# w_out's rows placed on eight DMA engines, and 13 gMLP chunks instead of 20

## The chip, the cores and the metric

One NeuronCore of one Trainium2 chip runs the whole kernel. The metric is the device time of one execution in microseconds, as the median of several runs.

## What is computed

Two branches share one input `x` (4 sequences, one token each, 640 wide), and their results are added to it. Everything is bf16 at the borders.

```python
def _A_ref(x, k_cache, v_cache, wq, wo):             # 32 heads of 128, 4096 keys, 4 sequences
    q = (x @ wq).reshape(B, Sq, H, Dh).transpose(0, 2, 1, 3)
    scores = einsum('bhqd,bhkd->bhqk', q, k_cache) * Dh ** -0.5
    o = einsum('bhqk,bhkd->bhqd', softmax(scores), v_cache)
    return o.transpose(0, 2, 1, 3).reshape(B, Sq, H * Dh) @ wo
def _B_ref(x, w_in, w_sp, b_sp, w_out):              # w_in 640 x 1728, w_out 864 x 640
    z = gelu(x @ w_in); z1 = z[..., :Fh]; z2 = layernorm(z[..., Fh:])
    g = einsum('ts,bsf->btf', w_sp, z2) + b_sp[None, :, None]
    return (z1 * g) @ w_out
x = A_x; xn = layernorm(x)
return x + _A_ref(xn, A_k_cache, A_v_cache, A_wq, A_wo) + _B_ref(xn, B_w_in, B_w_sp, B_b_sp, B_w_out)
```

The caches are 134 MB each, so nearly all of the work is reading them.

## The kernel before

**Memory.** `kv` is one SBUF tile of five slots; a slot holds half of a unit of K or V. A unit is one sequence and eight heads: 64 KB on each of 128 partitions, 8 MB in all, so that there are 16 units of K and 16 of V, four of each to a group of heads (g = 0 to 3). Slots 0 to 2 first hold the small weights: `wq` (slots 0 and 1), `w_in` and the first part of `w_out` (slot 2), with the scratch of the layernorm, of q and of the gMLP behind them. `w_words` is a second tile; it takes the transposed K blocks (two buffers of 2048 words, `kT_t`), and at the start, in the same words, the rest of `w_out` (`w_rest`).

**Loads.** SP issues all large loads in one written order: `wq`, `w_in`, `w_out` (lines 126 and 127), two of the three pieces of the rest of `w_out` (line 133), then the units K0, K1, K2, K3, V0, K4, V1, K5 and so on (line 181, the list `seq`), with `wo` of group 0 behind K7 and the other groups' `wo` at the end (line 189). The fourth K unit of each group and the last V unit come in two parts. `place` gives each unit its slots: K0 slots 3 and 4, K1 0 and 1, K2 2 and 3, K3 4 and 0, V0 1 and 2, later V units 0 and 1. SP waits before each issue until the slots are free, and the loads behind wait with it.

**The rest of w_out.** `w_out` has 864 rows of 640. The first 384 lie on all 128 partitions, three rows (FA) to a partition. The other 480 are cut into the pieces of `PC`: first partition, last partition, rows to a partition n, and a count k, the outermost dimension of the source, which sets on how many DMA engines the load runs. Pieces 0 and 1 go out on SP's queue with k = 5 and 3, piece 2 on GpSimd's queue (POOL) with k = 2. The engines of a GpSimd load are consecutive ones behind those of the GpSimd load before it; the load `walk` (14 rows of 256 elements into a tile that nothing reads) only moves that place on by seven. `tc.issue_after` keeps the order of the two. The unused partitions of `w_rest` are set to zero by the memset of line 128, for which the pieces wait.

**The gMLP at the start.** The layernorm of x (lines 205 to 222; GpSimd squares in L211), q (L301) and z = x w_in (L338 to L343, PSUM tiles `z_ps` and `zr_ps`) follow one another. `z` is laid out so that its columns match the rows of `w_out` on each partition and each chunk, a Gelu to each piece (L357 to L360). Then GpSimd and VectorE compute the inner layernorm and the gate (L371 to L390), and PE multiplies chunk by chunk (L403): FC = FA + FR = 20 chunks of 128 rows, two matmuls each, into `proj`, where the attention's output is added later. A chunk's matmul reads one row of `w_out` of every partition.

**Attention.** For each K unit VectorE transposes eight blocks into `w_words` (L425) and PE makes the scores (L436). Behind a group's fourth K unit come softmax, the fill of the block-diagonal weights `Zb` (L469 to L473), and for each V unit 64 matmuls (L509). The output projection with `wo` (L552) ends with the pieces of the last group's `wo`, then two small stores.

Of the kernel before, what the change touches and what calls it, by code (L numbers as in the profile page):

```python
# [1 line left out]

# [9 lines left out]
F32 = mybir.dt.float32  # L12
# [4 lines left out]
def kernel(  # L17
# [19 lines left out]
    nc = tc.nc  # L37
    P = 128
    B, Sq, D = A_x.shape
    _, H, Sk, Dh = A_k_cache.shape  # L40
    assert Sq == 1 and B == 4 and Dh == P and D % P == 0
    DC = D // P
# [11 lines left out]
    G = HG * B  # L54
    F2 = B_w_in.shape[1]
    Fh = F2 // 2
    FA = 3
    FR = 17
    nf = FA * P

    PC = ((0, 20, 10, 5), (32, 44, 12, 3), (60, 68, 17, 2))
    f_at = [nf]
    for p0, p1, n, _ in PC:
        f_at.append(f_at[-1] + (p1 - p0) * n)
    assert Fh == f_at[-1]
    FC = FA + FR
    NOUT = A_wo.shape[1]
# [11 lines left out]
    ps_o = ctx.enter_context(tc.tile_pool(name="ps_o", bufs=2, space=bass.MemoryType.PSUM))  # L79
# [6 lines left out]
    def misc_ps(shape, dtype):  # L86
        misc_ctr[0] += 1
        return ps_m.tile(shape, dtype, tag="misc", name=f"misc{misc_ctr[0]}")
# [5 lines left out]
    n_p = (2 * TC + 1) * 16  # L94
    w_words = const.tile([P, max(2 * NKT + n_p, FR * NOUT // 2)], F32, name="w_words")
    kT_t = w_words[:, 0:2 * NKT].rearrange("p (i n) -> p i n", i=2)
    pT_t = w_words[:, 2 * NKT:2 * NKT + n_p].bitcast(BF16).rearrange("p (j r) -> p j r", r=32)

    def at_slot(i, n, off=0):
        return kv[:, i * SL + off:i * SL + off + n]  # L100
# [22 lines left out]

    w_out = at_slot(2, FA * NOUT, n_in).rearrange("p (c n) -> p c n", c=FA)

    nc.sync.dma_start(out=w_out[:, 0:2], in_=B_w_out[0:2 * P, :].rearrange("(p c) n -> p c n", p=P))
    nc.sync.dma_start(out=w_out[:, 2:3], in_=B_w_out[2 * P:nf, :].rearrange("(p c) n -> p c n", p=P))
    nc.vector.memset(w_words[:, 0:FR * NOUT // 2], 0.0)  # L128
    w_rest = w_words[:, 0:FR * NOUT // 2].bitcast(BF16).rearrange("p (c n) -> p c n", c=FR)

    def load_piece(eng, t):
        p0, p1, n, k = PC[t]
        return eng.dma_start(out=w_rest[p0:p1, 0:n].rearrange("p c n -> p (c n)"),
                             in_=B_w_out[f_at[t]:f_at[t + 1], :].rearrange("(r i c) n -> i r (c n)", i=k, c=n))

    NST = 256
    walk = const.tile([14, NST], BF16)

    load_piece(nc.sync, 0)
    load_piece(nc.sync, 1)  # L140
    sw = nc.gpsimd.dma_start(out=walk, in_=B_w_out[0:14, 0:NST].rearrange("(r i) n -> i r n", i=7))
    with tc.issue_after(sw.ins):
        load_piece(nc.gpsimd, 2)

    NB = 32 * FC
    z_at = n_in + FA * NOUT

# [72 lines left out]
    xnT = const.tile([P, DC, 32], BF16)  # L220
# [43 lines left out]
    for q in range(4):  # L264
        nc.gpsimd.tensor_copy(out=SelE[32 * q:32 * q + 32, :, q % 2, :],
                              in_=b8[32 * q:32 * q + 32, 8:8 + HP, None].to_broadcast((32, HP, P // HG)))
# [10 lines left out]
                          in_=ident_f[:].rearrange("p (q x c) -> p q x c", q=2, c=C2))  # L277
# [12 lines left out]
    for hf in range(NH):  # L290
        nc.tensor.matmul(proj[0:32, 0:NO2], lhsT=ident_bf[:XR, 1 - hf:33 - hf],
                         rhs=x_bf[:, hf * NO2:(hf + 1) * NO2], start=(hf == 0), stop=False)
# [4 lines left out]
    for hf in range(2):  # L297
        for c in range(DC):
            for j in range(NG):
                n0 = j * HG * Dh + hf * 512  # L300
                nc.tensor.matmul(q4_ps[32 * j:32 * j + 32, hf * 512:hf * 512 + 512], lhsT=xnT[:, c, :],  # L301
                                 rhs=wq[:, c, n0:n0 + 512], start=(c == 0), stop=(c == DC - 1))
# [14 lines left out]
    w_z = w_in.rearrange("p c (a f) -> p c a f", a=2)  # L317
    z_ps = misc_ps([P, 2, FA, 32], F32)
    zr_ps = misc_ps([P, 2, 256], F32)


    z_in = [[], [], [], []]
    for t, (p0, p1, n, k) in enumerate(PC):
        src = w_z[:, :, :, f_at[t]:f_at[t + 1]]
        for q in range(p0 // 32, (p1 - 1) // 32 + 1):
            x0, x1 = max(p0, 32 * q), min(p1, 32 * q + 32)
            if x1 - x0 < p1 - p0:
                assert (x1 - x0) * k == p1 - p0
                src_q = src.rearrange("p d a (r i c) -> p d i a r c", i=k, c=n)[:, :, (x0 - p0) // (x1 - x0)]
            else:  # L330
                src_q = src
            z_in[q].append((t, x0 - 32 * q, x1 - 32 * q, src_q))
    z_of = [[sum((x1 - x0) * PC[t][2] for t, x0, x1, _ in z[:m]) for m in range(len(z) + 1)] for z in z_in]
    w_z2 = w_z[:, :, :, 0:2 * P].rearrange("p c a (q j i) -> p c q a i j", q=4, j=32)
    w_z1 = w_z[:, :, :, 2 * P:nf].rearrange("p c a (q j) -> p c q a j", q=4)
    for c in range(DC):
        for q in range(4):
            nc.tensor.matmul(z_ps[32 * q:32 * q + 32, :, 0:2], lhsT=xnT[:, c, :], rhs=w_z2[:, c, q], start=(c == 0), stop=False)  # L338
            nc.tensor.matmul(z_ps[32 * q:32 * q + 32, :, 2], lhsT=xnT[:, c, :], rhs=w_z1[:, c, q], start=False,
                             stop=(c == DC - 1))  # L340
        for q in range(4):
            for m, (_, _, _, src) in enumerate(z_in[q]):
                nc.tensor.matmul(zr_ps[32 * q:32 * q + 32, :, z_of[q][m]:z_of[q][m + 1]], lhsT=xnT[:, c, :], rhs=src[:, c],  # L343
                                 start=(c == 0 and m == 0), stop=(c == DC - 1 and m == len(z_in[q]) - 1))
    z_f = at_slot(2, 2 * 3 * NB, z_at).bitcast(F32).rearrange("p (a n) -> p a n", a=3)
    z_b = at_slot(2, 2 * NB, z_at + 6 * NB).rearrange("p (a n) -> p a n", a=2)
    zT = z_f[:, 0:2, :].rearrange("p a (i j) -> p a i j", j=32)
    nc.gpsimd.memset(z_f[:, 0:2, :], 0.0)
    nc.scalar.activation(out=zT[:, :, 0:FA, :], in_=z_ps[:], func=ACT.Gelu_apprx_tanh)
    for q in range(4):  # L350
        rows = slice(32 * q, 32 * q + 32)
        for m, (t, x0, x1, _) in enumerate(z_in[q]):
            p0, p1, n, k = PC[t]
            z = zr_ps[rows, :, z_of[q][m]:z_of[q][m + 1]]
            dst = zT[rows, :, FA:FA + n, x0:x1]
            if x1 - x0 < p1 - p0:
                nc.scalar.activation(out=dst, in_=z.rearrange("p a (x c) -> p a c x", c=n), func=ACT.Gelu_apprx_tanh)  # L357
            else:
                for a in range(2):
                    nc.scalar.activation(out=dst[:, a].rearrange("p c (i r) -> p c i r", i=k),  # L360
                                         in_=z[:, a].rearrange("p (r i c) -> p c i r", i=k, c=n), func=ACT.Gelu_apprx_tanh)
# [36 lines left out]
    for f0 in range(0, FC, 4):  # L398
        for hf in range(NH):
            for fc in range(f0, min(f0 + 4, FC)):  # L400
# [3 lines left out]
                                 rhs=(w_out[:, fc] if fc < FA else w_rest[:, fc - FA])[:, hf * NO2:(hf + 1) * NO2],  # L404
                                 start=(fc == 1 and hf == 0), stop=False)
# [156 lines left out]
    for i, item in enumerate(seq):  # L562
# [10 lines left out]
        g, b = divmod(u, B)  # L573
# [22 lines left out]
    for c, hf in ((0, 0), (1, 0), (0, 1), (1, 1), (2, 0), (2, 1)):  # L596
        p = min(c, 1)
# [49 lines left out]
```

## Time and profile before

| what | value |
|---|---|
| median of 3 runs | 663.61 us (663.38 to 663.67) |
| span of the profiled execution, first to last instruction | 661.8 us |
| its own launch time | not listed apart; 1.8 us lie between the span and the median |
| DMA: packets, bytes, mean rate | 7132, 282.60 MB, 427 GB/s |
| PE, VectorE, ScalarE, GpSimd busy | 43%, 57%, 11%, 11% |
| mean granted TensorE clock | 0.736 |
| PE's code fetches (q8 instruction) | 18, 0.29 MB |

Queue q1 in the profile is SP's, q10 ScalarE's, q0 GpSimd's; q8 and q14 bring instructions. The DMA row of the page gives the busy tenths of all 16 DMA engines in 40 slices of 16.5 us. In the chain of work each step is followed back to what released it. Beside the views, the trace holds a record for every DMA packet (queue, start, duration, bytes), though not its engine; where the text speaks of packet records, these are meant.

### The profile page before, as it was taken

Reading aid. Unit: us, or ns where it says so; the run is one execution under the profiler, and the core shown is the slowest. Engines: PE = TensorE matmul, PEld = TensorE weight load, DVE = VectorE, ACT = ScalarE, POOL = GpSimd, SP = SyncE. Lnnn points to the kernel's source line nnn. Section 1 sums busy time; section 2 is a strip of 40 time slices with the busy share of each in tenths; the row PEclk is TensorE's granted clock in tenths of the full one; section 3 lists DMA queues with packets and bytes.
Section 4 is the critical chain, followed back from the end, with each engine's and each line's share of the span. In section 5 each row is a group of like instructions: output and inputs, shape, how many; then the busy total and the mean of one; then the engine's idle time right before and its main releaser. Section 6 shows DMA issues by size and latency. Waiting matters only on the chain.

```text
span 661.8 us, 5507 instructions
## 1 busy us (share of the span) xinstructions
PE 286.8 (43%) x2291; PEld 107.4 (16%) x2291; DVE 377.1 (57%) x307; ACT 74.0 (11%) x143; POOL 70.1 (11%) x138
## 2 busy tenths in 40 slices
PE   0336555446052456234426065642607245541236
PEld 0221111112011122111102022210202112120113
DVE  5329989766191759718346196764619175971112
ACT  0300000340100000330200000070100000042200
POOL 4620000030200000130300000030110000002300
PEclk9868788669578596676858587665857768766678
DMA  9999999999999999999999999999999999999997
GB/s 370 457 429 428 427 442 437 440 421 428 421 440 433 440 415 446 425 437 436 437 432 432 429 418 437 446 433 440 425 420 436 437 436 417 456 420 437 419 420 289
DMA packets 7132, 282.60 MB, mean 427 GB/s; under 512 B 913, under 2 KB 1308, under 8 KB 1692
## 3 DMA queue, kind: packets, MB, share of 16 engines
q1 hardware_dynamic: 6968, 282.07, 98.9%
q8 instruction: 18, 0.29, 0.2%
q0 software_dynamic: 112, 0.18, 0.1%
q14 instruction: 6, 0.05, 0.0%
q10 hardware_dynamic: 28, 0.01, 0.0%
HBM read 282.25 MB, written 0.01 MB: 426 GB/s over the span
## 4 chain that ended last, share of the span: by engine, by line
DMA 75%; DVE 11%; issue 11%; PE 2%; DVEq 0%; SPq 0%
DMA kv<-in_A_k_cache_dram 59%; DVE w_words L425 11%; DMA kv<-in_A_v_cache_dram 10%; DMA kv<-in_A_wo_dram 4%; DMA kv<-in_A_wq_dram 3%; PE O L509 2%; PE S L436 0%; PE proj L552 0%; DVE o_q L604 0%; DVE o L600 0%; DVEq L425 0%; SPq L189 0%; DVE o_bf L615 0%; SPq L181 0%; PE last L552 0%
## 5 line engine op out<-in xcount | busy, mean ns | idle before, releaser
L425 DVE STREAM_TRANSPOSE w_words<-kv 128x2048 f32<-128x2048 f32 x128 | 282.8, 2275 | 124.8 <-DMA kv<-in_A_k_cache_dram 124.8
L436 PE MATMUL S<-w_words,QZ 128*32 128x512 bf16 x1024 | 186.1, 496 | 258.3 <-DVE w_words L425 258.3
L436 PEld LDWEIGHTS <-QZ 128*32 128x32 bf16 x1024 | 59.7, 110 | 382.9 <-issue 319.5
L509 PE MATMUL O<-kv,Zb 128*32 128x512 bf16 x1024 | 75.0, 458 | 57.4 <-DMA kv<-in_A_v_cache_dram 50.8
L473 ACT ACTIVATE Zb<-w_words,MkE 32x128 bf16<-32x128 bf16 x120 | 61.0, 508 | 117.9 <-PE O L509 104.2
L518 DVE TENSOR_TENSOR om<-O,Mk 128x512 f32<-128x512 f32 x15 | 10.4, 692 | 94.6 <-PE O L509 94.6
L471 POOL TENSOR_SCALAR Zb<-w_words,MkE 32x128 bf16<-32x128 bf16 x60 | 43.1, 718 | 139.3 <-PE O L509 126.9
L509 PEld LDWEIGHTS <-Zb 128*32 128x32 bf16 x1024 | 34.0, 113 | 98.4 <-issue 70.3
L485 ACT ACTIVATE p_bf<-S,negmax 128x1024 bf16<-128x1024 f32 x4 | 4.5, 1114 | 401.8 <-DVE negmax L453 401.8
L469 DVE TENSOR_SCALAR Zb<-w_words,MkE 32x128 bf16<-32x128 bf16 x76 | 24.7, 325 | 2.3
L411 POOL COPY QZ<-qT 32x32 bf16<-32x32 bf16 x16 | 5.0, 315 | 186.4 <-PE S L436 185.9
L519 DVE TENSOR_REDUCE R<-om 128x128 f32<-128x512 f32 x15 | 15.3, 1020 | 0.5
L496 POOL TENSOR_SCALAR rs<-MkB,rowsum 128x4 f32<-128x4 f32 x4 | 1.2, 296 | 112.4 <-ACT p_bf L485 112.4
L491 DVE STREAM_TRANSPOSE w_words<-p_bf 128x1024 bf16<-128x1024 bf16 (+1 forms) x8 | 9.6, 1241 | 5.9 <-ACT p_bf L485 4.1
L542 POOL MEMSET oT<- 128x66 bf16 x4 | 0.5, 146 | 96.5 <-PE proj L552 96.5
L443 DVE TENSOR_REDUCE m<-S 128x1 f32<-128x1024 f32 x4 | 4.9, 1224 | 6.1 <-PE S L436 6.1
L521 DVE TENSOR_SCALAR R<-O,Mk 128x128 f32<-128x128 f32 x1 | 0.4, 351 | 14.0 <-PE O L509 14.0
L531 PE MATMUL misc<-R,SelX 128*128 128x512 f32 x8 | 4.5, 644 | 7.2 <-DVE R L519 5.5
L301 PE MATMUL q<-kv,xnT 128*32 128x512 bf16 x40 | 4.3, 617 | 6.4 <-DVE xnT L222 6.4
L498 PE MATMUL misc<-rs,SelE 128*128 128x4 f32 x8 | 2.4, 365 | 10.4 <-POOL rs L496 10.4
L128 DVE MEMSET w_words<- 128x5440 f32 x1 | 4.6, 4592 | 1.9 <-issue 1.9
L534 DVE TENSOR_TENSOR om<-misc,h 128x512 f32<-128x512 f32 x4 | 2.8, 692 | 4.9 <-PE misc L531 4.9
(107 smaller groups left out, 88.2 us busy)
## 6 DMA issues: line engine op xcount, KB each, us to landing
kv<-in_A_k_cache_dram SPq DMA_DIRECT2D x8, 4096.0 KB, 30.2
kv<-in_A_v_cache_dram SPq DMA_DIRECT2D x1, 6144.0 KB
kv<-in_A_wq_dram SPq DMA_DIRECT2D x1, 5120.0 KB, 16.8
kv<-in_A_wo_dram SPq DMA_DIRECT2D x3, 1280.0 KB
kv<-in_B_w_in_dram SPq DMA_DIRECT2D x1, 2160.0 KB, 22.3
kv<-in_A_v_cache_dram SPq DMA_DIRECT2D x1, 2048.0 KB
kv<-in_A_wo_dram SPq DMA_DIRECT2D x1, 640.0 KB, 23.6
kv<-in_B_w_out_dram SPq DMA_DIRECT2D x1, 320.0 KB
```

The source lines that it names most:

```text
L128: nc.vector.memset(w_words[:, 0:FR * NOUT // 2], 0.0)
L411: nc.gpsimd.tensor_copy(out=QZ[r0:r0 + 32, :, :, :, 8 + 8 * hp], in_=qT[32 * g:32 * g + 32, NE * hp:NE * hp + NE].rearrange("p e a b -> p ...
L425: nc.vector.transpose(kT.rearrange("p (t r) -> p t r", r=32), kw)
L436: nc.tensor.matmul(S_ps[32 * q:32 * q + 32, i], lhsT=QZ[:, b, 2 * kh + w, e, w0:w0 + 32], rhs=kb[:, i, :, e, :, w], start=(b == 0 and k < ...
L443: nc.vector.tensor_reduce(out=m1[:], in_=S_ps[:].rearrange("p i t m -> p (i t m)"), axis=AX.X, op=ALU.max)
L469: nc.vector.tensor_scalar(out=dst, in0=src, scalar1=mk, scalar2=None, op0=ALU.mult)
L471: nc.gpsimd.tensor_scalar(out=dst, in0=src, scalar1=mk, scalar2=None, op0=ALU.mult)
L473: nc.scalar.activation(out=dst, in_=src, func=ACT.Copy, scale=mk)
L491: nc.vector.transpose(pT_t[:, j0:j1, :], blocks)
L509: nc.tensor.matmul(O_ps[32 * q:32 * q + 32, :, :], lhsT=Zb[b % 2][:, w].rearrange("p h c -> p (h c)"), rhs=vv[:, w * 4 * Dh:(w + 1) * 4 * ...
L518: nc.vector.tensor_tensor(out=om4[:], in0=O_ps[:], in1=Mk4[:, :, None].to_broadcast((P, 4, Dh)), op=ALU.mult)
L519: nc.vector.tensor_reduce(out=R, in_=om4[:].rearrange("p c d -> p d c"), axis=AX.X, op=ALU.add)
```

## The change

The part of `w_out` that lies on all partitions shrinks from three rows to one (FA = 1, so each DMA engine brings 8 rows of it). The other 736 rows go into seven pieces of 12 or 11 rows to a partition (FR = 12). The first two (k = 5) are on SP's queue, 92 rows on each of five engines; one with k = 2 and four with k = 1 are on GpSimd's queue, with three more walks between them that place each on the engine wanted. So that a load runs on one engine alone, the source of a k = 1 piece is read in another order (`fold`), row by row, and z and its Gelu follow that order. There are 13 chunks instead of 20. z needs a third PSUM tile, `zx_ps`, for the columns of GpSimd's pieces, and `z_ps` shrinks with FA.

```diff
@@ -54,11 +54,13 @@
     G = HG * B
     F2 = B_w_in.shape[1]
     Fh = F2 // 2
-    FA = 3
-    FR = 17
+    FA = 1
+    FR = 12
     nf = FA * P
 
-    PC = ((0, 20, 10, 5), (32, 44, 12, 3), (60, 68, 17, 2))
+    PC = ((0, 20, 12, 5), (32, 52, 11, 5), (60, 68, 12, 2), (92, 96, 12, 1), (28, 32, 11, 1), (96, 100, 11, 1),
+          (124, 128, 11, 1))
+    NHW = 2
     f_at = [nf]
     for p0, p1, n, _ in PC:
         f_at.append(f_at[-1] + (p1 - p0) * n)
@@ -123,24 +125,34 @@
 
     w_out = at_slot(2, FA * NOUT, n_in).rearrange("p (c n) -> p c n", c=FA)
 
-    nc.sync.dma_start(out=w_out[:, 0:2], in_=B_w_out[0:2 * P, :].rearrange("(p c) n -> p c n", p=P))
-    nc.sync.dma_start(out=w_out[:, 2:3], in_=B_w_out[2 * P:nf, :].rearrange("(p c) n -> p c n", p=P))
+    nc.sync.dma_start(out=w_out, in_=B_w_out[0:nf, :].rearrange("(p c) n -> p c n", p=P))
     nc.vector.memset(w_words[:, 0:FR * NOUT // 2], 0.0)
     w_rest = w_words[:, 0:FR * NOUT // 2].bitcast(BF16).rearrange("p (c n) -> p c n", c=FR)
 
+    def fold(n):
+        return 3 if n % 3 == 0 else n
+
     def load_piece(eng, t):
         p0, p1, n, k = PC[t]
-        return eng.dma_start(out=w_rest[p0:p1, 0:n].rearrange("p c n -> p (c n)"),
-                             in_=B_w_out[f_at[t]:f_at[t + 1], :].rearrange("(r i c) n -> i r (c n)", i=k, c=n))
+        src = B_w_out[f_at[t]:f_at[t + 1], :]
+        if k > 1:
+            src = src.rearrange("(r i c) n -> i r (c n)", i=k, c=n)
+        else:
+            src = src.rearrange("(j i) n -> i j n", i=fold(n))
+        return eng.dma_start(out=w_rest[p0:p1, 0:n].rearrange("p c n -> p (c n)"), in_=src)
 
     NST = 256
     walk = const.tile([14, NST], BF16)
 
-    load_piece(nc.sync, 0)
-    load_piece(nc.sync, 1)
-    sw = nc.gpsimd.dma_start(out=walk, in_=B_w_out[0:14, 0:NST].rearrange("(r i) n -> i r n", i=7))
-    with tc.issue_after(sw.ins):
-        load_piece(nc.gpsimd, 2)
+    def load_walk(k):
+        return nc.gpsimd.dma_start(out=walk[0:2 * k, :], in_=B_w_out[0:2 * k, 0:NST].rearrange("(r i) n -> i r n", i=k))
+
+    for t in range(NHW):
+        load_piece(nc.sync, t)
+    sw = None
+    for step in (("w", 7), ("p", 2), ("w", 6), ("p", 3), ("w", 7), ("p", 4), ("p", 5), ("w", 6), ("p", 6)):
+        with (tc.issue_after(sw.ins) if sw is not None else nullcontext()):
+            sw = load_walk(step[1]) if step[0] == "w" else load_piece(nc.gpsimd, step[1])
 
     NB = 32 * FC
     z_at = n_in + FA * NOUT
@@ -317,6 +329,7 @@
     w_z = w_in.rearrange("p c (a f) -> p c a f", a=2)
     z_ps = misc_ps([P, 2, FA, 32], F32)
     zr_ps = misc_ps([P, 2, 256], F32)
+    zx_ps = ps_o.tile([P, 2, 256], F32, tag="O", name="zx")
 
 
     z_in = [[], [], [], []]
@@ -329,19 +342,29 @@
                 src_q = src.rearrange("p d a (r i c) -> p d i a r c", i=k, c=n)[:, :, (x0 - p0) // (x1 - x0)]
             else:
                 src_q = src
+            if k == 1:
+                src_q = src.rearrange("p d a (j i) -> p d a i j", i=fold(n))
             z_in[q].append((t, x0 - 32 * q, x1 - 32 * q, src_q))
-    z_of = [[sum((x1 - x0) * PC[t][2] for t, x0, x1, _ in z[:m]) for m in range(len(z) + 1)] for z in z_in]
-    w_z2 = w_z[:, :, :, 0:2 * P].rearrange("p c a (q j i) -> p c q a i j", q=4, j=32)
-    w_z1 = w_z[:, :, :, 2 * P:nf].rearrange("p c a (q j) -> p c q a j", q=4)
+    z_at_q = []
+    for z in z_in:
+        used = [0, 0]
+        z_at_q.append([])
+        for t, x0, x1, _ in z:
+            w, b = (x1 - x0) * PC[t][2], int(t >= NHW)
+            z_at_q[-1].append(((zr_ps, zx_ps)[b], used[b], used[b] + w, used[b] == 0))
+            used[b] += w
+        assert max(used) <= 256
+    w_z1 = w_z[:, :, :, 0:nf].rearrange("p c a (q j) -> p c q a j", q=4)
     for c in range(DC):
         for q in range(4):
-            nc.tensor.matmul(z_ps[32 * q:32 * q + 32, :, 0:2], lhsT=xnT[:, c, :], rhs=w_z2[:, c, q], start=(c == 0), stop=False)
-            nc.tensor.matmul(z_ps[32 * q:32 * q + 32, :, 2], lhsT=xnT[:, c, :], rhs=w_z1[:, c, q], start=False,
+            nc.tensor.matmul(z_ps[32 * q:32 * q + 32, :, 0], lhsT=xnT[:, c, :], rhs=w_z1[:, c, q], start=(c == 0),
                              stop=(c == DC - 1))
         for q in range(4):
             for m, (_, _, _, src) in enumerate(z_in[q]):
-                nc.tensor.matmul(zr_ps[32 * q:32 * q + 32, :, z_of[q][m]:z_of[q][m + 1]], lhsT=xnT[:, c, :], rhs=src[:, c],
-                                 start=(c == 0 and m == 0), stop=(c == DC - 1 and m == len(z_in[q]) - 1))
+                zt_ps, o0, o1, lead = z_at_q[q][m]
+                last_of = m == len(z_in[q]) - 1 or z_at_q[q][m + 1][3]
+                nc.tensor.matmul(zt_ps[32 * q:32 * q + 32, :, o0:o1], lhsT=xnT[:, c, :], rhs=src[:, c],
+                                 start=(c == 0 and lead), stop=(c == DC - 1 and last_of))
     z_f = at_slot(2, 2 * 3 * NB, z_at).bitcast(F32).rearrange("p (a n) -> p a n", a=3)
     z_b = at_slot(2, 2 * NB, z_at + 6 * NB).rearrange("p (a n) -> p a n", a=2)
     zT = z_f[:, 0:2, :].rearrange("p a (i j) -> p a i j", j=32)
@@ -351,9 +374,10 @@
         rows = slice(32 * q, 32 * q + 32)
         for m, (t, x0, x1, _) in enumerate(z_in[q]):
             p0, p1, n, k = PC[t]
-            z = zr_ps[rows, :, z_of[q][m]:z_of[q][m + 1]]
+            zt_ps, o0, o1, _ = z_at_q[q][m]
+            z = zt_ps[rows, :, o0:o1]
             dst = zT[rows, :, FA:FA + n, x0:x1]
-            if x1 - x0 < p1 - p0:
+            if k == 1 or x1 - x0 < p1 - p0:
                 nc.scalar.activation(out=dst, in_=z.rearrange("p a (x c) -> p a c x", c=n), func=ACT.Gelu_apprx_tanh)
             else:
                 for a in range(2):
```

More of the change, by code (lines that the diff above doesn't have):

```diff
@@ L1 @@
-from contextlib import ExitStack
+from contextlib import ExitStack, nullcontext
 import concourse.bass as bass
```

## The prediction, made before the changed kernel was run

> **What bounds the kernel now.** I read the page first, its sections 2 to 4.
>
> ```profile
> DMA  9999999999999999999999999999999999999997
> q1 hardware_dynamic: 6968, 282.07, 98.9%
> q0 software_dynamic: 112, 0.18, 0.1%
> DMA 75%; DVE 11%; issue 11%; PE 2%; DVEq 0%; SPq 0%
> ```
>
> The 16 DMA engines are busy in every slice, nearly all of it with SP's queue (q1). So only two things lengthen the run: an engine that gets more to do than the others, and a moment when SP cannot issue the next load in time. The second is read from the chain in order of time and from VectorE's timeline:
>
> ```profile
> 17.55 27.97 DMA kv<-in_A_k_cache_dram
> 45.74 2.37 DVE w_words L425 x2
> 54.64 0.02 SPq L181
> 54.76 29.47 DMA kv<-in_A_k_cache_dram
> ```
>
> ```profile
> 45.74 17.66 DVE L425 STREAM_TRANSPOSE w_words<-kv 128x2048 f32<-128x2048 f32 x8 [7.52 <-DMA kv<-in_A_k_cache_dram]
> 65.00 17.66 DVE L425 STREAM_TRANSPOSE w_words<-kv 128x2048 f32<-128x2048 f32 x8 [1.60 <-DMA kv<-in_A_k_cache_dram]
> 84.42 35.20 DVE L425 STREAM_TRANSPOSE w_words<-kv 128x2048 f32<-128x2048 f32 x16 [1.76 <-DMA kv<-in_A_k_cache_dram]
> ```
>
> Unit K0 lands at about 45.5, VectorE transposes it, and after four of its eight transposes SP may issue K2 (54.76), which overwrites them. By the packet records the fastest engines have finished K1 at 59.55 and the slowest at 64.4, so K2's issue is some 5 us early for the fastest. At 134.90 it is not early enough: V1 is issued 15.28 us after the last transpose of group 0 (84.42 + 35.20 = 119.62), and the records show the fast engines dry at 137.0, their next packets ending as if begun at 138.1 to 139.1. The transposes write `w_words`, where the rest of `w_out` lies until the gMLP's chunk matmuls have read it; PE's timeline has these end at 43.1, 2.6 us before K0 lets VectorE start:
>
> ```profile
> 39.06 4.06 PE L403 MATMUL proj<-w_words,kv 128*8 128x320 bf16 x33
> ```
>
> Last, the DMA view of two stretches, the one up to 9 us with the walk alone on GpSimd's queue (q0), the one from 9 to 19.6 us with its piece:
>
> ```profile
> q0 software_dynamic: 32, 0.01, 0.4%
> ```
>
> ```profile
> q0 software_dynamic: 80, 0.17, 4.2%
> ```
>
> 32 is 16 x 2 and 80 is 16 x 5. The walk has two runs of 512 bytes for each of seven engines: the records show one packet of 1024 bytes on each, one of 8 bytes on the nine others, and a semaphore packet on all 16. The piece has four runs of 21760 bytes for each of two engines: four packets there, four of 4 bytes on the 14 others, and a semaphore packet on all. So a GpSimd load is complete only when every engine has taken all its turns. And the turns alternate: in the records one q0 packet comes after one q1 packet, however long that is (on the two data engines 11.63, 13.94, 16.26, with wq packets of 1.51 us between).
>
> **The change part by part.**
>
> *Fewer chunks.* 14 of 40 chunk matmuls go (38.28 to 43.12, so 0.121 each, 1.7 us); memset 5440 to 3840 columns (4.59 to 3.24 us); GpSimd's gMLP steps on 640 columns (1.16, 1.25, 2.51, 0.87, 1.53) shrink to 416, some 2.2 us, VectorE's (0.82, 0.82, 0.84) by 0.9; against that ScalarE gets 4 Gelu pieces more (0.27 each, 1.1). Some 3.7 us shorter, worth nothing on the path: K0's landing covers it. One SP load less before K0 is worth nothing either: K0's first packet starts behind `w_out` at about 21 us in any case.
>
> *Rows moved between engines.* From the rows: a 1280-byte packet costs 0.052 us, one of 15360 bytes 0.570 (0.0475 a row), one of 12800 0.476, the eight of 2560 together 0.80. Engines 0 to 2 go from 112 rows to 100: -0.80 + 0.19 = -0.6 us. Engines 3 and 4 go from 64 to 100: 4 x 0.476 becomes 4 x 0.570 + 4 x 0.523, so +2.47 - 0.80 = +1.7. Engines 7 and 8: about +0.3 to +0.5. Engine 15: 92 x 0.0475 to 0.052 - 0.80 = +3.6 to +4.0. The eight others: -0.8. I followed each engine's semaphore packets from load to load. It ends at 653.9 on one that carries few rows and takes no code fetch (I take it for 15); 655.6 and 657.8 on 3 and 4; 656.1 and 656.5 on 7 and 8; 657.3 to 658.1 on 0 to 2; 656.0 to 657.9 on the eight that share the 16 KB code fetches (about 1.5 us each). The later of 3 and 4 takes three 8 KB fetches of about 1 us each. So alone this moves the latest end from 658.1 to 657.8 + 1.7 + 0.2 (more q0 packets) = 659.7: +1.6. The eight's 0.8 is not gained: they wait at 137 us anyway.
>
> *Five pieces and four walks on GpSimd.* (a) GpSimd's own time: the walk's issue took 0.80 us, the piece's 0.57. The four single-engine pieces have 44 or 48 runs instead of 8: each between 0.57 and 0.57 x 6 = 3.4. With three walks and the first piece the run of issues is 5.3 to 16.6 us from about 5.4 on. The idle 4.99 us before L211 hides part, so the layernorm, q and the gMLP come 0 to 11 us later; 2.6 + 3.7 us of cover stands behind it. I take 2 us each, hidden. (b) What queues: every engine gets 2 + 5 + 2 + (N+1) + 2 + (N+1) + (N+1) + 2 + (N+1) q0 packets, N being the packets of a 44- or 48-row piece. N does not show in the trace. The ends: one run of 1280 to a packet (48) and, since two runs of 21760 were not put together, at most 33 (2 packets). The nearest row is the walk's 512-byte runs, two to a packet: N = 24 and 22. After 9 us q0 needs 15 + 4N turns. Beside it SP's queue has, on an engine without its own pieces, 3 wq packets and a semaphore, 9 for w_in, 9 for w_out by 20.2 us, then 9 for K0 to 40 us and 9 for K1 to 59.5: 40. N = 2 needs 23 (lands near 23 us), N = 4 needs 31 (near 41), and from N = 7 on it needs over 40: q0 is still waiting for turns when SP's queue has run dry behind K1.
>
> The Trainium skill ("DMA: Bandwidth & Descriptors", SWDGE vs HWDGE vs iDMA) gives a packet as at most 4096 bytes preferably and at most 64 descriptors, and as the boundary at which an engine changes queue; by it three runs share a packet, N is 16 or 15, 76 turns are needed, and the sum comes out as the one below. The walk's 1024-byte packets agree; the 21760-byte ones show that a longer run is not cut.
>
> *What the late piece holds up.* Every chunk matmul from L403 on reads all 128 partitions of `w_rest`, so PE stands at the second chunk until the last piece is there; behind it are all S matmuls, and VectorE's first transpose, which overwrites `w_rest`; behind that SP's K2. This is a ring: K2 cannot refill the queue before the piece has landed, and the piece has its turns only once the queue is dry.
> - The last piece lands with K1's slowest engine: 64.4 - 0.6 + 0.4 for q0's packets, about 64.3; PE sees it at 65.0 (K0's last packet to VectorE's start took 0.67).
> - 16 matmuls free the first transpose: 2.0, and 0.3 to hand over: VectorE starts K0 at 67.3, not 45.74 (+21.6).
> - K2 is issued 9.0 later, at 76.3, with all engines idle since 59.2 to 64.3.
> - VectorE then runs 32 transposes of 2.207 without its waits of now: 67.3 + 70.6 = 137.9, not 119.62: +18.3.
> - V1 is issued 15.3 later, at 153.2, effective at 156.4 to 157.4. Data does not come later: K2 effective at about 79, four 19.33 us loads, 156.3.
> - From V1 on all is as before, 18.3 later, but engines start it level, so the latest end is that of the code-fetching ones (4.05 after the first, where the latest was 4.26): -0.2.
>
> Sum: +18.1 on the span of 661.8, 679.9. Median less span is 1.8 before; kept, it makes 681.6.
>
> **The rivals.**
> 1. *Packets large or early enough* (N of 4 or less): the gMLP is done in time and only the rows count: the engine of 3 and 4 with three fetches ends last, +1.6, 665.2. For it: nothing in the trace excludes up to 33 runs to a packet. Against: the one q0 packet with several runs holds 1024 bytes.
> 2. *Partly late* (N of 5 or 6, or GpSimd's issues at their upper end of 3.4 us): VectorE starts 5 to 15 us late, of which 3 are slack: 667 to 678.
> 3. *Not slower*: pieces early as in 1, and the three fetches fall on an engine with slack (my numbering of engines 3, 4 and 15 rests on following packets whose order crosses at 137 us). Then the code-fetching eight set the end, 4.05 against 4.26: 663.4. It decides against me if q0's pieces land before 38 us and no engine with 100 rows ends after 658.1.
> 4. *Faster*: as 3, and the eight's 0.8 survives 137 us because V1 is issued earlier by as much (its chain starts with K2's slowest engine, 0.6 earlier). 662.6 would be within 0.2%; over 1.3 us also needs the fetches to spread better.
>
> **How the numbers follow.** The likeliest is the ring at 681.6, chance 0.70: all N from 7 to 48 give nearly the same time; its own range is 679 to 684 (start-up of an idle queue, 1.6 to 4.2 us after the issue in the two places seen, the start and V1). Rival 2 has 0.08, rival 1 0.10, rival 3 0.07, rival 4 0.05. The range reaches down to rival 1: 664.9 to 684. 0.2% (1.3 us) is what a measurement tells from no change: slower 0.88, same 0.07, faster 0.05.
>
> **What would show it.** In the changed profile: VectorE's first L425 at about 67 released by PE, not by K0's landing at 45.7; L403 on `w_words` at 65, waiting for w_out's DMA; SP's third K issue near 76; DMA slices 4 and 5 of the page (50 to 83 us) far below 9; hundreds of small q0 packets, some 80 an engine; the GpSimd pieces' time to landing near 50 us. The prediction is wrong if the first transpose still starts near 46: then N is small, and the end decides between rivals 1 and 3.

## The result and the profile after

The changed kernel takes 670.42 us (median of 4 runs, 669.46 to 671.43), the kernel before 663.5 beside it: 1.0102 times as long, interval 1.0088 to 1.0117, or 6.9 us more. The profiled execution took 671.43 us, its span is 669.3, 7.5 more than before. The forecast was 681.6. Of the executions behind the ratios below, one is left out: one of four of the run with one packet and the walks as in the change took 681.40 us, and no trace of it was kept.

The page after, the lines that answer to the first fence of the prediction:

```profile
DMA  9989999999999999999999999999999999999996
q1 hardware_dynamic: 6834, 281.89, 98.0%
q0 software_dynamic: 992, 0.39, 0.2%
DMA 71%; issue 14%; DVE 12%; PE 3%; POOL 0%; DVEq 0%; SPq 0%; POOLq 0%
```

Apart from the last, only one slice is below 9 (33 to 50 us); the ring of the forecast would have left two far below. 992 is 16 x 62: the "some 80 an engine" are 62.

The chain of waits, in order of time, up to VectorE's first transpose:

```profile
1.39 7.94 DMA walk<-in_B_w_out_dram
9.62 9.61 DMA walk<-in_B_w_out_dram
19.52 9.60 DMA walk<-in_B_w_out_dram
29.41 0.57 POOL walk L148
30.01 24.66 DMA w_words<-in_B_w_out_dram
54.71 2.05 PE proj L427 x14
56.78 2.37 DVE w_words L449 x2
```

In the kernel before this chain was SP's loads, ending with K0. Now it is walk behind walk on GpSimd's queue. GpSimd's timeline says why (start, duration, what, and in brackets the idle time before it and what ended that):

```profile
9.62 0.56 POOL L148 DMA_DIRECT2D walk<-in_B_w_out_dram  x1 [3.88 <-DMA walk<-in_B_w_out_dram]
19.52 0.56 POOL L148 DMA_DIRECT2D walk<-in_B_w_out_dram  x1 [8.48 <-DMA walk<-in_B_w_out_dram]
29.41 0.60 POOL L148 DMA_DIRECT2D walk<-in_B_w_out_dram  x1 [7.56 <-DMA walk<-in_B_w_out_dram]
30.01 0.90 POOL L142 DMA_DIRECT2D w_words<-in_B_w_out_dram  x1
31.29 1.24 POOL L223 TENSOR_TENSOR kv<-kv 8x640 f32<-8x640 f32 x1
```

All four walks write the same tile `walk`, so each but the first waits until the one before it has landed: 3.88 + 8.48 + 7.56 = 19.9 us in which GpSimd stands. Behind the last one is the layernorm's square (L223, L211 before), at 31.29 instead of 12.88. Behind the square are q, the transposed `qT` and GpSimd's copies of it; K1 overwrites the scratch of these, so SP's queue waits too. SP's timeline, and VectorE's:

```profile
43.13 23.00 SPq L193 DMA_DIRECT2D kv<-in_A_k_cache_dram  x2
```

```profile
56.78 70.29 DVE L449 STREAM_TRANSPOSE w_words<-kv 128x2048 f32<-128x2048 f32 x32 [3.33 <-PE proj L427]
```

K1 is issued at 43.13 instead of 25.1, when by the packet records K0's fastest engine has been finished for 3.1 us. The windows of the trace (after the engines' busy times: granted clock, DMA share, GB/s) show the hole:

```profile
30.00:39.00 9.00, 2.83 (x28) 1.08 (x32) 3.08 (x7) 0.29 (x1) 8.41 (x31) 1.00 1.10 468
39.00:44.00 5.00, 3.21 (x77) 2.03 (x69) 2.10 (x3) 2.74 (x7) 4.23 (x18) 1.00 0.52 188
44.00:56.00 12.00, 2.31 (x14) 1.34 (x16) 2.26 (x6) 4.50 (x11) 5.08 (x7) 0.59 1.08 440
```

In that hole GpSimd's packets hardly have to take turns with SP's; the DMA view of 39 to 44 us:

```profile
q1 hardware_dynamic: 24, 0.85, 41.0%
q0 software_dynamic: 319, 0.06, 8.2%
```

So the pieces come in behind K0, not behind K1. PE's timeline has the gMLP ready at 53.5 and the last piece hardly later:

```profile
53.51 0.43 PE L427 MATMUL proj<-kv 128*8 128x320 bf16 x1 [5.77 <-DVE kv L414]
54.71 0.69 PE L427 MATMUL proj<-w_words,kv 128*32 128x320 bf16 x3 [0.77 <-DMA w_words<-in_B_w_out_dram]
```

The wait for the piece is short. In the packet records the pieces' last data packet ends at 46.0; what is still out are three packets on GpSimd's queue, two of 16 bytes and a semaphore packet, which by their times (49.30, 51.75, 54.21) stand on one engine, each right behind a packet of K1. VectorE starts 3.33 us after its last step of the gMLP (L414); in the run with useless work below, where PE waits for no piece, it is 2.44. So some 0.9 us of VectorE's delay is the piece's, and the rest comes of the late layernorm.

From there the sum closes. VectorE starts 56.78 - 45.74 = 11.04 us late, runs its 32 transposes without the two waits of before (1.60 and 1.76) and 0.23 faster for not stopping, and ends them at 127.07, 7.45 late. V1 is issued at 142.33, 7.43 late; the span is 7.5 longer.

### The profile page after: what moved, and what is told of

Read it like the earlier page. It is cut to its first block, busy times and chain, and to the rows that moved or that the text cites. A ratio compares the mean times of both kernels' runs of the same rounds, so it can differ in the third digit from the quotient of the medians.

```text
span 669.3 us, 5493 instructions
## 1 busy us (share of the span) xinstructions
PE 279.3 (42%) x2277; PEld 106.0 (16%) x2277; DVE 374.8 (56%) x307; ACT 74.5 (11%) x147; POOL 72.9 (11%) x145
## 4 chain that ended last, share of the span: by engine, by line
DMA 71%; issue 14%; DVE 12%; PE 3%; POOL 0%; DVEq 0%; SPq 0%; POOLq 0%
DMA kv<-in_A_k_cache_dram 49%; DVE w_words L449 12%; DMA kv<-in_A_v_cache_dram 10%; DMA walk<-in_B_w_out_dram 4%; DMA w_words<-in_B_w_out_dram 4%; DMA kv<-in_A_wo_dram 4%; PE O L533 2%; PE proj L427 0%; PE S L460 0%; PE proj L576 0%; DVE o_q L628 0%; POOL kv L113 0%; POOL walk L148 0%; DVE o L624 0%; DVEq L449 0%
## 5 line engine op out<-in xcount | busy, mean ns | idle before, releaser
L460 PE MATMUL S<-w_words,QZ 128*32 128x512 bf16 x1024 | 181.2, 485 | 255.6 <-DVE w_words L449 255.6
L533 PE MATMUL O<-kv,Zb 128*32 128x512 bf16 x1024 | 72.9, 448 | 58.8 <-DMA kv<-in_A_v_cache_dram 55.6
L576 PE MATMUL proj<-kv,oT 128*8 128x320 bf16 x54 | 5.6, 350 | 1.1 <-DMA kv<-in_A_wo_dram 1.1
```

What stands on the lines that cost most here:

```text
L460: nc.tensor.matmul(S_ps[32 * q:32 * q + 32, i], lhsT=QZ[:, b, 2 * kh + w, e, w0:w0 + 32], rhs=kb[:, i, :, e, :, w], start=(b == 0 and k < ...
L533: nc.tensor.matmul(O_ps[32 * q:32 * q + 32, :, :], lhsT=Zb[b % 2][:, w].rearrange("p h c -> p (h c)"), rhs=vv[:, w * 4 * Dh:(w + 1) * 4 * ...
L576: nc.tensor.matmul(dst[0:nb, 0:n1 - n0], lhsT=state[("oT", g)][:, c0:c0 + nb], rhs=wo_t[g][:, c, n0:n1], start=start, stop=stop)
```

## The experiments

The kernel before beside the first four runs: 663.57 us; beside the later ones 663.50 to 663.51. In brackets stand the ratio to it and the ratio's interval. The theory after the result: the walks' waits made K1 late and so let the pieces in early; without the waits the forecast's ring comes back. The rival: the waits are the whole loss, and without them the change costs the rows or nothing.

**Walks in columns of their own.**

```diff
-    walk = const.tile([14, NST], BF16)
+    walk = const.tile([14, 4 * NST], BF16)
...
+        return nc.gpsimd.dma_start(out=walk[0:2 * k, c0:c0 + NST], ...)
```

Here `c0` moves on by 256 columns from walk to walk.

> The changed kernel, but every walk writes columns of its own, so that no walk waits for the walk before it and GpSimd issues all its loads by about 12 us. Theory (waits and turns are two causes): without the waits the layernorm is back at about 13 us and K1 is issued near 25 us, so SP's queue no longer runs dry behind K0; the pieces still take 12 or 13 turns each on every engine (60 turns against some 40 of SP's queue up to the end of K1), so the last piece lands only behind K1, near 64 us, the first transpose starts near 67, and the time is 679 to 684: slower than the change. Rival (the walk waits are the whole loss): the first transpose starts near 46 and the time is 663.5 to 665.5.

681.47 us (1.0274, 1.0258 to 1.0289): 11 us longer without the waits. From the chain in order of time, PE's timeline, the page, VectorE's timeline and the windows:

```profile
37.55 0.43 PE proj L430
37.98 28.25 another core or an unknown queue
```

```profile
66.27 0.69 PE L430 MATMUL proj<-w_words,kv 128*32 128x320 bf16 x3 [28.29 <-DMA w_words<-in_B_w_out_dram]
```

```profile
DMA  9996499999999999999999999999999999999996
```

```profile
68.34 70.29 DVE L452 STREAM_TRANSPOSE w_words<-kv 128x2048 f32<-128x2048 f32 x32 [30.85 <-PE proj L430]
```

```profile
58.00:78.00 20.00, 9.24 (x56) 3.70 (x58) 9.65 (x5) 0.00 (x0) 0.00 (x0) 0.58 0.17 68
```

This is the ring: PE is ready at 37.98 and stands 28.25 us for the last piece; engines are nearly idle from 58 to 78 us (0.17); the first transpose, forecast at 67.3, starts at 68.34, and the time is the forecast's 681.6 to 0.1. So close a total is partly luck: V1 is issued 0.4 us later than forecast (153.56), and the span is 0.4 shorter (679.5). In the packet records the last piece's packets, one of 5120 bytes every 2.64 us, alternate with K's packets of 2.42.

**One packet for a small piece.** The same with `single_packet=(k == 1)` on the pieces.

> As the kernel with walks of their own, and each single-engine piece is one packet (44 or 48 runs together), so that it takes two turns on every engine. Both theories: all pieces land by about 25 us, the first transpose starts near 46 released by K0's landing. What is left is the row placement alone. Theory of the prediction: the later of engines 3 and 4, with three code fetches, sets the end, +1.6 us: 665.2. Rival (the placement does even the ends out, or costs nothing): 662.5 to 663.8.

682.09 us (1.0276, 1.0261 to 1.0292). The records still show packets of 5120 bytes, so the option did nothing and the run is a repeat of the one above: it says nothing of the theories.

**The walks alone.** The kernel before, with three more walks into the same tile behind its piece, and the square behind them:

```diff
+    for k in (6, 7, 6):
+        with tc.issue_after(sw.ins):
+            sw = nc.gpsimd.dma_start(out=walk[0:2 * k, :], ...)
...
+    with tc.issue_after(sw.ins):
+        nc.gpsimd.tensor_tensor(out=sq, in0=xc, in1=xc, op=ALU.mult)
```

> The kernel before, with three more walks into the same tile behind its one GpSimd piece, and the square of the layernorm behind them on GpSimd: the waits alone, without the new pieces, rows or chunks. Theory: each walk waits for the landing of the walk before it, the square starts near 30 us instead of 12.9, K1 is issued near 42, the first transpose starts near 58, and the time is about 672. Rival (the pieces' turns are the loss, the waits cost nothing): 663.5.

673.14 us (1.0141, 1.0126 to 1.0156). GpSimd's and VectorE's timelines:

```profile
20.81 0.55 POOL L146 DMA_DIRECT2D walk<-in_B_w_out_dram  x1 [8.04 <-DMA walk<-in_B_w_out_dram]
30.02 0.54 POOL L146 DMA_DIRECT2D walk<-in_B_w_out_dram  x1 [7.00 <-DMA walk<-in_B_w_out_dram]
```

```profile
57.22 70.29 DVE L430 STREAM_TRANSPOSE w_words<-kv 128x2048 f32<-128x2048 f32 x32 [3.19 <-PE proj L408]
```

With the old rows, chunks and pieces the waits alone put the first transpose at 57.22 and cost as much as the whole change. Here too the late gMLP alone holds VectorE: PE's chunk matmuls run from 54.09 without a wait for `w_out`. By the medians it is even 2.7 us longer than the changed kernel, but the two profiled executions are only 0.3 apart (671.72, the shortest of its four, and 671.43, the longest of its four), with first transposes 0.44 apart; the other executions have no trace.

**One packet, walks as in the change.**

> The changed kernel with its walks as they are (one tile, each waiting for the walk before), but each single-engine piece is one packet. Theory: the walks still wait for turns behind K0's packets of 2.4 us, the square starts at 27 to 30 us instead of 31.3, the pieces land before the gate is ready, and the first transpose starts near 54 instead of 56.8: about 668. Rival (the pieces' turns are the whole loss): 663.5 to 665.5.

669.99 us (1.0091, 1.0071 to 1.0111), packets unchanged: a repeat of the changed kernel, within its runs.

**A GpSimd that is merely late.** If what matters is when K1 joins SP's queue, useless work should do what the waits do. Walks in their own columns, 22 memsets behind the last piece, and the square behind these:

```diff
+    for i in range(22):
+        with tc.issue_after(sw.ins):
+            sw = nc.gpsimd.memset(Zb[i % 2]..., 0.0)
```

> The kernel with walks in columns of their own (681.5) and 22 memsets of 128x1024 (0.95 us each) on GpSimd between its last piece and the layernorm's square; they write zeros where zeros are written anyway. No walk waits for a landing; GpSimd is merely late by about as much as in the changed kernel. Theory (the order of K1's issue and of the pieces' turns decides: if K1 comes to SP's queue late, the queue is dry behind K0 and the pieces drain there): square near 32 instead of 13.1, K1 issued near 43 instead of 25, the last piece landed near 50, first transpose near 56 to 58 instead of 68.3, 669 to 674, that is some 10 us faster by 20 us of useless work. Rival (the pieces' own turns or landings are slow wherever K1 stands, or the walks' waits themselves paced the pieces): 681 or more, the delay of GpSimd added or hidden.

670.55 us (1.0106, 1.009 to 1.0121), 10.9 less than without the memsets. GpSimd's, SP's, PE's and VectorE's timelines:

```profile
11.05 19.75 POOL L162 MEMSET Zb<- 128x1024 f32 x22
32.97 1.24 POOL L232 TENSOR_TENSOR kv<-kv 8x640 f32<-8x640 f32 x1 [1.65 <-DVE kv L230]
```

```profile
44.48 22.12 SPq L200 DMA_DIRECT2D kv<-in_A_k_cache_dram  x2
```

```profile
54.86 0.43 PE L431 MATMUL proj<-kv 128*8 128x320 bf16 x1 [5.77 <-DVE kv L418]
55.18 0.69 PE L431 MATMUL proj<-w_words,kv 128*32 128x320 bf16 x3
```

```profile
57.25 70.29 DVE L453 STREAM_TRANSPOSE w_words<-kv 128x2048 f32<-128x2048 f32 x32 [2.44 <-PE proj L431]
```

GpSimd waits 0.24 us for a walk here, and K1's issue, the first transpose and the time are those of the change within 1.4, 0.5 and 0.2 us. With K1 late the pieces are in (their last packet ends at 46.3 in the records) before PE asks for them at 55.18, as against 66.27 with K1 early. What then holds VectorE is the late gMLP alone. So one delay of GpSimd does two things: it lets the pieces in behind K0, and it makes the gMLP late. No run has K1 late and the gMLP early.

**Few turns, no waits between walks: what the rows cost.** Three layouts kept the 100 rows on engines 0 to 4 and 13 chunks and took away the walks' waits for each other and the small packets. First, five walks in columns of their own, and the single-engine pieces cut into runs of 3 to 6 rows on four engines each:

```diff
-    ... (92, 96, 12, 1), (28, 32, 11, 1), (96, 100, 11, 1), (124, 128, 11, 1))
+    ... (92, 96, 12, 4), (28, 32, 12, 4), (96, 100, 12, 4), (124, 128, 9, 4))
```

> The changed kernel with its walks in columns of their own (no walk waits for another) and its four single-engine pieces cut into long runs instead: 12, 12, 12 and 9 rows for each of four partitions, in runs of 6 rows (7680 bytes; 3 rows, 3840 bytes, in the last), which go to four engines each, 2 or 3 packets apiece. Engines 0 to 4 keep their 100 rows; the rest lies elsewhere than in the changed kernel. Every engine gets about 28 turns of GpSimd's queue instead of 60. Theory (the loss is turns and the walk-to-walk wait, and the rows are the small rest): the layernorm's square is back near 13, K1 is issued near 25, the last piece has landed by about 32, VectorE's first transpose is released by K0 near 45.7, V1 is issued near 135, and only the 100 rows on engines 3 and 4 remain: 665.2 (664.3 to 666.2). Rival A (100 rows on 3 and 4 cost nothing, since those engines have slack): 663.5. Rival B (something else in the change, as the second PSUM bank or the smaller gMLP, holds the 7 us): 669 to 671.

667.45 us (1.0058, 1.0045 to 1.007), over the range of the theory. K0 releases the first transpose, at 47.29, so the gMLP is off the path; but GpSimd waited again (8.83 us, the last section has the rows), and the packet records show SP's packets some 20% longer from 16 to 27 us, summed up 1.8 us an engine. Second, one walk and two pieces, the second on five engines:

```diff
-    ... (92, 96, 12, 1), (28, 32, 11, 1), (96, 100, 11, 1), (124, 128, 11, 1))
+    ... (96, 111, 12, 5))
```

> The changed kernel with 100 rows on each of engines 0 to 4 and 13 chunks, but GpSimd's queue as short as in the kernel before: one walk, the piece for engines 7 and 8 (4 packets of 15360 bytes each), and the remaining 180 rows in one piece of five engines (3 packets of 15360 bytes each), some 11 turns on every engine. No second walk, so nothing for GpSimd to wait for; no small runs. It tells the rows by themselves, which the run with few turns left open at 667.45 (there the packets of all engines between 16 and 27 us took some 20% longer, about 1.9 us an engine, which no theory had). Theory (rows on engines 3 and 4 cost the 1.6 us of the prediction, the rest of that run was the slow stretch): 665.2 (664.3 to 666.0), no slow stretch. Rival A (the rows cost 3.9, the slow stretch nothing): 667 to 668. Rival B (rows cost nothing, the latest end is on another engine): 663.5.

667.02 us (1.0048, 1.0034 to 1.0061), with the slow stretch, against the theory. The same window in this run and in the kernel before:

```profile
14.50:20.00 5.50, 0.71 (x8) 0.42 (x12) 2.74 (x7) 0.29 (x1) 4.91 (x21) 1.00 1.04 282
```

```profile
14.50:20.00 5.50, 2.24 (x24) 0.90 (x28) 2.73 (x7) 0.29 (x1) 4.91 (x21) 1.00 0.98 417
```

From the five-engine piece's first packet (15.0) to its last (21.4) nearly all w_in packets take 0.9 to 1.1 us instead of 0.644: 2.1 us an engine for SP's packets, and 2.5 with GpSimd's own. Third, the same rows in pieces of two engines:

```diff
-    ... (96, 111, 12, 5))
+    ... (96, 104, 12, 2), (108, 120, 7, 2))
```

> As the run with three loads (100 rows on engines 0 to 4, one walk, no waits), but the rows that GpSimd loads go two engines at a time: 96 rows on engines 7 and 8, 96 on the next two, 84 on the two after (runs of 15360, 15360 and 8960 bytes), some 19 turns an engine. In the run with three loads every engine's w_in packets took 0.9 to 1.1 us instead of 0.644 from the first to the last packet of the five-engine piece (15.0 to 21.4 us), some 2.4 us an engine; in the run with four-engine pieces it was 1.9. Theory (that stretch comes of a GpSimd piece on four or five engines at once, and the 100 rows on engines 3 and 4 cost 1.6): no slow stretch, w_in packets at 0.644, 665.2 (664.4 to 665.9). Rival A (the stretch comes with any GpSimd data on engines other than 7 and 8, or beside w_in): 666.5 to 668 with slow w_in packets. Rival B (the rows cost nothing): 663.5 without slow packets.

666.11 us (1.004, 1.0026 to 1.0053), just above the range. The stretch is short now, 0.9 us an engine for SP's packets; V1 is issued at 134.41, 0.5 earlier than before, and the last engine ends its loads at 660.56, 2.46 later than before's last. Taking SP's slow packets off the profiled execution in which they were measured gives 667.27 - 1.8 = 665.5, 667.82 - 2.1 = 665.7 and 666.22 - 0.9 = 665.3 us (the recorded expectations have 1.9 and 2.4 for the first two stretches). These are 1.7 to 2.1 us above the 663.61 of the kernel before's profiled execution, near the 1.6 us of the prediction for the rows, but by subtraction: no run had the rows without slow packets, and the records, which hold no engine, do not show that engines 3 and 4 end last. Why a GpSimd piece on several engines slows all sixteen is open.

## Why the prediction was wrong

**The step that failed** is (a) of "Five pieces and four walks on GpSimd". It priced the issues (2 us for each single-engine piece; they took 0.82 to 0.90) and called them hidden. It left out that walks two to four wait for the landing of the walk before, since they write one tile. The trace of the kernel before had the price, in its DMA view (KB, us from issue to landing):

```profile
walk<-in_B_w_out_dram POOLq DMA_DIRECT2D x1, 7.0 KB, 7.9
```

Three such landings one behind the other are 24 us; the changed kernel took 7.94, 9.61 and 9.60. Who is queued behind was named ("the layernorm, q and the gMLP") with a delay of 0 to 11 us; it was 18.4, beyond the 2.6 + 3.7 us of cover, and SP's K1, which waits for q's scratch, was not followed at all.

**What that did to the ring.** Its mechanism was right: without the waits it came out at 68.34 and 681.47 us. With K1 18 us late, SP's queue ran dry one unit earlier, and the pieces found their turns behind K0. "Lands with K1's slowest engine at 64.3" became about 54.2, VectorE's start 56.78 instead of 67.3, the end of group 0's transposes +7.45 instead of +18.3, V1 +7.43 instead of +18.3, the sum +7.5 instead of +18.1. What is left of the loss is no small ring: it is the late layernorm, with some 0.9 us of the piece. The waits turned a loss of 18 us into one of 7; taking them away alone makes the kernel slower.

**N was mis-sized**, 24 and 22 where the records show packets of 5120 bytes, four runs of 1280, hence 12 and 11. That changed nothing in the sum, as the prediction said for all N from 7 on. Its sign "some 80 an engine" does not follow from its own N: with the walks and the first piece, 24 and 22 make 107 packets, and 12 and 11 the measured 62. The Trainium skill ("DMA: Bandwidth & Descriptors", SWDGE vs HWDGE vs iDMA) prefers packets of at most 4096 bytes, which by an estimate from that figure would make N 16 and 15. The measured 5120 decide. The Trainium skill (the same page, Queues, rings and completion order) has each engine take turns between queues at packet boundaries. The 2.64 us from one 5120-byte packet to the next with walks apart, a K packet of 2.42 between, agree.

**Rows.** The +1.6 on engines 3 and 4 is near what the subtraction leaves, 1.7 to 2.1, but is not shown on these engines. In the changed kernel it cannot be seen: eleven of its engines have finished K0 by 43.7 us and begin K1 anew, and the 7.43 us of V1 make up its 7.5. **Fewer chunks** cost and gained nothing where K0 releases VectorE, as forecast: the three layouts start it at 46.2 to 47.8. In the changed kernel the gMLP is on the path and its shortness helps: from the square to the first transpose it takes 25.5 us, some 0.9 of them the piece's, against 26.5 with 20 chunks (the walks alone). **Rivals:** "partly late" named the right size (667 to 678) by luck, from other causes, pieces half early or issues of 3.4 us each; its 0.08 was far too low, because every case was built on N or the issues and none on when SP issues K1.

## What to carry to other kernels

A dummy load that only places a queue still writes somewhere: two of them into one tile make the issuing engine wait for a landing, and everything behind it on that engine, and whoever waits for that, is late. Where two queues share engines packet by packet, a small load lands when it has had its turns, and when it gets them depends on when the long queue is next empty; so ask of every delay which load it moves across which dry stretch. Before mending a wait, price the kernel without it: here the wait hid the larger loss.

## What the runs showed of the hardware

- A load on GpSimd's queue whose data goes to one engine gives the others as many packets of 16 bytes as that engine has packets of 5120: the changed kernel's records hold 45 of 5120 bytes and 675 (45 x 15) of 16. All GpSimd loads together make 62 turns on each engine, most of them without data.
- With ten GpSimd loads to separate places (few turns), GpSimd stood before the ninth and the tenth until a walk and a piece had landed, 0.81 and 8.02 us, which we take for the first and the second load. Whether the chip or the compiled program asks for this is open. Its timeline:

```profile
9.97 0.55 POOL L156 DMA_DIRECT2D walk<-in_B_w_out_dram  x1 [0.81 <-DMA walk<-in_B_w_out_dram]
18.54 0.62 POOL L147 DMA_DIRECT2D w_words<-in_B_w_out_dram  x1 [8.02 <-DMA w_words<-in_B_w_out_dram]
```

- GpSimd pieces on four or five engines beside w_in's load slowed the packets of all sixteen engines (282 against 417 GB/s with five); pieces on two engines did so less (w_in's packets took 0.694 us in the mean against 0.644), those on one engine hardly (0.651).
